# Moving 64 channels of the last convolution block to GpSimd, two halves at a time

## The chip, the cores and the metric

The kernel runs on one core of a Trainium2 chip. The metric is the device time of one execution in microseconds (us). The engines of the core run their own instruction streams in order and wait for each other through semaphores: TensorE (PE in the profile, its weight loads PEld), VectorE (DVE), ScalarE (ACT), GpSimd (POOL) and SyncE (SP), which here only issues DMAs.

## The reference

```python
# x: (8, 3904, 192), weight: (8 heads, 7 taps), w1, w2: (192, 1024), w3: (1024, 1024), w_out: (1024, 192)
w = softmax(weight)                                  # over the 7 taps of a head
x_pad = 6 zero rows ahead of each batch's 3904 rows
conv[b, s, h, g] = sum_k w[h, k] * x_pad[b, s + k, h, g]   # a causal convolution, 24 channels a head
out = ((conv @ w1) * (conv @ w2)) @ w3 @ w_out       # for all 31232 rows
```

## The kernel before, in words

**Tiling.** The 31232 rows are cut into two streams of 15616 (`NS = 2`), and each stream into 31 *rounds* of 512 columns (`CH`). The convolved x of a round is held transposed, with channels on partitions: three chunks `k = 0, 1, 2` of 64 channels, both streams stacked to 128 partitions. w3 and w_out are multiplied once at the start, so that a round has only two products:

- `first_product(R)` (L581): in 8 steps `ft` of 128 columns of w1 and w2, TensorE makes `pa` and `pb` (L596), ScalarE casts `pa` to `asb` (L603) and VectorE multiplies it by `pb` into `abT` (L605).
- `second_product(R, r)` (L615): for one stream, 32 matmuls into `ops` (L621), copied by ScalarE to `osb` (L626) and stored by SyncE (L635).

All PSUM results take turns in four tiles of two banks (`banks`).

**Stages.** Three rounds make a stage (the loop `for p, (rounds, ends)`, L863): first the three first products (24 steps), then the six second products, numbered `n = 0..5`. Other work is written into this order by hand. Two stages more at the end deal with the last rounds.

**Two ways to convolve.** Two rounds, 2q+1 and 2q+2, are a *pair* (`phase_of`, L56).

- *On TensorE*, for the pairs that are not in `SIDE`: x is loaded in blocks of windows (`x_jobs`, L137, DMAs of L158), multiplied by a banded matrix `Aband` in units of two heads (`conv`, L310, matmuls L328), evicted by ScalarE (L337), stored to DRAM as `rows` (`store`, L370) and read back by DMA transposes (`transposes`, L422). Blocks 4, 5 and 6 have 80 windows and four units each. `places` (L731) says after which second product of which stage a unit runs: `{0: (1, 2, 3, 4), 2: (0, 1, 3, 4), 4: (2, 4), 5: (1, 3)}`. Block 6, for the pairs 10 and 11, is in stages 4 and 5. x rows ahead of a batch are zeroed by GpSimd (`clear`, L857, memsets L860) once the x loads of a tile have been issued.
- *Beside it*, for the pairs in `SIDE`: a GpSimd DMA casts one chunk of x to `rows_c` (`side_cast`, L473, DMA L480), SyncE transposes it to `raw` (L489), and the seven taps are summed in fp32. Most of it is VectorE's: ScalarE makes the first product (`side_first`, L492), and VectorE adds six taps, one instruction each (`side_sums`, L498, L512), in the second half of a stage, `rooms` (L732) giving about how many sums a stage holds. Seven half-chunks of 512 columns are GpSimd's (`BY_POOL`, L450).

**GpSimd's halves.** Half number p of `BY_POOL` is cast in or before stage p, transposed by SyncE at the beginning of stage p's second half (`pool_transpose`, L531, L533) and summed in stage p + 1. `pool_sums` (L535) makes seven products (L539, `tensor_scalar`, the tap's weight a per-partition scalar; the first goes straight to `acc`) and six adds (L559, the last one L554). There is one `raw`, one `acc` and one `tmp`. The seven jobs are handed out one each to the `points` (L812) of a stage: a point (j, ft) lies behind step ft of the stage's round j, and GpSimd first makes a tiny copy `pace` from that step's abT (L876), so that it starts no sooner. Its DMAs (casts and x loads, `jobs`) are dealt to the same points by `counts` (L867).

**Queues.** An instruction that waits holds up all that is behind it on its engine. On SyncE, at the start of a second half, come transposes of `rows` that are due (`turn`), the side transposes of the next stage, GpSimd's transpose, and then the output stores; side transposes called `late` (L890) come after the output stores.

Of the kernel before, what the change touches and what calls it, by code (L numbers as in the profile page):

```python
# [8 lines left out]
FP32 = mybir.dt.float32  # L9
# [7 lines left out]
def kernel(  # L17
# [10 lines left out]
    nc = tc.nc  # L28
# [20 lines left out]
    SIDE = (4, 5, 8, 9, 12, 13, 14)  # L49
    SIZES = [20, 20, 20, 40, 80, 80, 80]  # L50
# [5 lines left out]
    def phase_of(R):  # L56
        return (R - 1) // 2

# [28 lines left out]
    def tok(i):  # L87
        return wins[i][0]

# [220 lines left out]
    def conv(b, c0, wd, evict=(nc.scalar.copy,), es=None):  # L310
        n, m, E = shape_of(b)
        es = range(E) if es is None else es
        if b not in convo_of:
            convo_of[b] = work.tile([128, n, NP, NS, Q], BF16, tag="convo", bufs=2,
                                    name="convo")
            left_of[b] = D * E
        convo = convo_of[b]
        cps = {e: banks("cps") for e in es}
        c = c0
        while c < c0 + wd:  # L320
            h = c // G
            c1 = min(h * G + G, c0 + wd)
            for j in range(4):
                xb, s = xb_of[b][j]
                for e in es:
                    for r in range(NS):
                        o = cps[e][j * C:j * C + C, r, 0:m * wd]
                        nc.tensor.matmul(  # L328
                            o.rearrange("p (w g) -> p w g", g=wd)[:, :, c - c0:c1 - c0],
                            Aband[group(r, e), h, :], xb[group(r, e), s:s + m, c:c1],  # L330
                            start=True, stop=True)
            c = c1
        for f, e in zip(evict, es):
            src = cps[e][:, :, 0:m * wd].rearrange("p r (w g) -> p r w g", g=wd)
            o = 0
            for k, lo, c in segments(c0, wd):
                f(out=convo[:, e::E, k, :, lo:lo + c]  # L337
                    .rearrange("p w r g -> p r w g"), in_=src[:, :, :, o:o + c])
                o += c
        left_of[b] -= wd * len(es)  # L340
        if not left_of[b]:
            del xb_of[b]
# [27 lines left out]
    def store(b, first=0, js=range(4)):  # L370
        n = SIZES[b] // 4
        convo = convo_of[b]
        for j in js:
            w = 0
            while w < n:
# [6 lines left out]
                elif s1 - s0 < ST:  # L382
                    m = 1
                    if s1:
                        nc.sync.dma_start(
                            out=rows[t + s0:t + s1, :],
                            in_=convo[C * j + s0:C * j + s1, w].rearrange("s k r g -> s (k r g)"))
                else:
                    src = convo[C * j:C * j + ST, w:w + m].rearrange("s w k r g -> s w (k r g)")
                    dst = rows[t:t + ST * m, :].rearrange("(w s) c -> s w c", s=ST)  # L390
# [31 lines left out]
    def transposes(R, first=0):  # L422
        t0, t1 = max(R * CH, first), min((R + 1) * CH, TS)
        a = ring_of[R] * CH % RING + t0 - R * CH
        for k in range(NP):
            nc.sync.dma_start_transpose(
                out=xT[k][:, a:a + t1 - t0], in_=rows[t0:t1, k * 128:(k + 1) * 128])
# [22 lines left out]
    BY_POOL = ((5, 2, 0), (5, 2, 1), (8, 2, 0), (8, 2, 1), (12, 2, 0), (12, 2, 1), (13, 2, 0))  # L450
# [69 lines left out]
    pool_raw, pool_acc, pool_tmp = [], [], const.tile([128, CH], FP32, name="tmp")  # L520

    def pool_tiles():
        t = stage.tile([128, 3 * CH + HALO], BF16, tag="wo", bufs=1, name="acc")
        pool_acc.append(t[:, 0:2 * CH].bitcast(FP32))
        pool_raw.append(t[:, 2 * CH:3 * CH + HALO])
# [5 lines left out]
    def pool_transpose(p, k, half):  # L531
        _, _, t0, _ = pool_half(p, k, half)
        nc.sync.dma_start_transpose(out=pool_raw[0], in_=rows_c[t0 - HALO:t0 + CH, k, :])  # L533

    def pool_sums(p, k, half):  # L535
        _, _, t0, starts = pool_half(p, k, half)

        def product(out, d):
            nc.gpsimd.tensor_scalar(  # L539
                out=out, in0=pool_raw[0][:, HALO - d:HALO - d + CH],  # L540
                scalar1=wC[:, k, K - 1 - d:K - d], scalar2=None, op0=ALU.mult)

        def job(d):
            def run():
                acc, tmp = pool_acc[0], pool_tmp
                if d == 1:
                    product(acc, 1)
                    for z in starts:
                        nc.gpsimd.memset(acc[:, z - t0:z - t0 + 1], 0.0)
                    return  # L550
                product(tmp, d)
# [10 lines left out]
        return [job(d) for d in list(range(1, K)) + [0]]  # L562

    def operand(R, k, rs):
        if phase_of(R) in side_of:
# [165 lines left out]
    places = {0: (1, 2, 3, 4), 2: (0, 1, 3, 4), 4: (2, 4), 5: (1, 3)}  # L731
# [43 lines left out]
    def later_loads():  # L775
# [9 lines left out]
        for i in starts[1]:  # L785
            for f in side_cast(i):
# [23 lines left out]
             for h in range(0, H, n)]  # L810
# [8 lines left out]
    pool_from = {p: v for p, v in enumerate(BY_POOL, 1)}  # L819
    pool_sum = {p + 1: pool_sums(*v) for p, v in pool_from.items()}  # L820
    casts = [(p - 1, f) for p in starts if p > 1 for i in starts[p] for f in side_cast(i)]
    casts += [(p, f) for p, (q, k, h) in pool_from.items()
# [40 lines left out]
    for p, (rounds, ends) in enumerate(phases):  # L863
# [3 lines left out]
        counts = [0] * 3 + [2] * 4 if p == 1 else [2] * 2 + [1] * 5  # L867
# [3 lines left out]
        for v, f in enumerate(pool_sum.pop(p, ())):  # L871
            at[v].append(f)
# [17 lines left out]
        late = [i for i in raws if p == 0 or i >= 5 and chain[p][0][0] <= i - 5]  # L890
# [55 lines left out]
```

## Time and profile before

| | us |
|---|---|
| runs | 511.17, 511.72, 512.06 (median 511.72) |
| the profiled execution | 510.92 |
| its span on the core | 509.2 |

The prediction shows lines of these views. *Engine totals*: busy us, share of the span and number of instructions of each engine. *The chain that ended last*: the work followed back from the last instruction, each step to what released it, as shares by engine, or as pieces in order of time (start, us, what). *Groups*: line, engine, operation, written tile <- read tiles, shapes, count | busy us, mean ns of one | idle us of the engine just before them and what ended that. *Timeline*: start, us from the first start to the last end of a run of like instructions, then the group, its count, and in brackets the idle time before it and who ended it. *DMA issues*: tile written <- tile read, queue, count, KB of one, median us from issue to landing.

### The profile page before, as it was taken

The numbers are of one execution on the slowest core, as the hardware profiler recorded it, in microseconds if no ns is written. First come the engines' busy times: TensorE is split into PE (matmuls) and PEld (weight loads), VectorE is DVE, ScalarE is ACT, GpSimd is POOL, SyncE is SP. The second block draws the span as 40 slices with busy tenths as digits, with TensorE's granted clock in tenths as the row PEclk, the third lists the DMA queues.
The fourth block names the chain that finished last, engine by engine and source line by source line (L and its number), as shares of the span: only waits on it lengthen the run. The fifth ranks groups of instructions, "written<-read, shape, count | busy, mean of one in ns | idle before, by whom it ended". The sixth has DMA issues, their size and how long they took to land.

```text
span 509.2 us, 13681 instructions
## 1 busy us (share of the span) xinstructions
PE 503.8 (99%) x5758; PEld 338.5 (66%) x5758; DVE 446.4 (88%) x402; ACT 347.2 (68%) x386; POOL 229.3 (45%) x303
## 2 busy tenths in 40 slices
PE   8999999999999999999999999999999999999997
PEld 4546864595569557845875596569557855965597
DVE  7898769999999799899989999999899999999930
ACT  6786667836778776477667767763776477457752
POOL 9966101333980597079519902970573067100000
PEclk9999999999999999999999999999999999999999
DMA  9999979999955999963889337975501400230024
GB/s 136 158 162 174 173 152 177 148 163 194 159 60 159 143 158 133 229 79 23 65 219 96 24 106 127 192 110 155 102 1 43 156 4 0 84 106 1 1 63 156
DMA packets 156825, 58.45 MB, mean 115 GB/s; under 512 B 112607, under 2 KB 156763, under 8 KB 156763
## 3 DMA queue, kind: packets, MB, share of 16 engines
q0 software_dynamic: 70560, 16.85, 37.2%
q1 hardware_dynamic: 86043, 40.62, 36.1%
q8 instruction: 45, 0.74, 0.6%
q14 instruction: 17, 0.14, 0.1%
q10 hardware_dynamic: 160, 0.10, 0.1%
HBM read 33.97 MB, written 34.85 MB: 135 GB/s over the span
## 4 chain that ended last, share of the span: by engine, by line
PE 98%; DMA 1%; ACT 0%; POOL 0%; DVE 0%; issue 0%; POOLq 0%
PE ops L621 32%; PE pa L596 31%; PE pb L596 31%; PE cps L328 1%; PE wps L693 1%; DMA xb<-in_x_dram 1%; PE tps L401 0%; PE ops L646 0%; PE tps L416 0%; DVE abT L605 0%; PE cps L357 0%; ACT asb L603 0%; POOL xb L158 0%; ACT convo L337 0%; ACT osb L650 0%
## 5 line engine op out<-in xcount | busy, mean ns | idle before, releaser
L605 DVE TENSOR_TENSOR abT<-asb,pb 128x1024 bf16<-128x1024 bf16 x240 | 292.7, 1221 | 30.4 <-ACT asb L603 14.5
L603 ACT CAST asb<-pa 128x1024 bf16<-128x1024 f32 x244 | 247.0, 1012 | 64.2 <-PE pa L596 64.0
L596 PEld LDWEIGHTS <-wn 64*128 64x128 bf16 x1488 | 138.5, 94 | 79.7 <-issue 1.6
L596 PEld LDWEIGHTS <-ws 64*128 64x128 bf16 x1488 | 129.7, 94 | 70.0 <-issue 1.4
L621 PE MATMUL ops<-W_sb,abT 128*128 128x192 bf16 x1936 | 163.7, 246 | 0.0
L621 PEld LDWEIGHTS <-abT 128*128 128x128 bf16 x1936 | 158.5, 98 | 6.4 <-issue 6.4
L596 PE MATMUL pb<-xT,wn 64*128 64x512 bf16 x408 | 111.2, 376 | 0.0
L596 PE MATMUL pa<-xT,wn 64*128 64x512 bf16 x408 | 110.1, 376 | 0.1
L596 PE MATMUL pa<-xT,ws 64*128 64x512 bf16 x408 | 110.1, 376 | 0.0
L596 PE MATMUL pb<-xT,ws 64*128 64x512 bf16 x408 | 108.5, 376 | 0.0
L626 ACT COPY osb<-ops 128x768 f32<-128x768 f32 (+1 forms) x61 | 48.5, 795 | 84.7 <-PE ops L621 82.3
L876 POOL COPY pace<-abT 1x2 bf16<-1x2 bf16 x57 | 10.9, 192 | 175.5 <-DVE abT L605 155.0
L596 PE MATMUL pb<-side,wn 64*128 64x512 bf16 (+1 forms) x336 | 88.8, 368 | 0.0
L596 PE MATMUL pa<-side,ws 64*128 64x512 bf16 (+1 forms) x336 | 87.3, 369 | 0.0
L596 PE MATMUL pa<-side,wn 64*128 64x512 bf16 (+1 forms) x336 | 87.3, 369 | 0.0
L512 DVE SCALAR_TENSOR_TENSOR acc<-raw,wC,acc 128x1024 f32<-128x1024 bf16 (+2 forms) x70 | 84.6, 1209 | 2.0
L596 PE MATMUL pb<-side,ws 64*128 64x512 bf16 (+1 forms) x336 | 85.7, 368 | 0.0
L539 POOL TENSOR_SCALAR tmp<-acc,wC 128x512 f32<-128x512 bf16 x42 | 65.8, 1566 | 1.2
L559 POOL TENSOR_TENSOR acc<-acc,tmp 128x512 f32<-128x512 f32 x35 | 44.4, 1267 | 2.9
L480 POOL DMA_DIRECT2D rows_c<-in_x_dram x50 | 37.1, 744 | 4.7 <-issue 2.7
L158 POOL DMA_DIRECT2D xb<-in_x_dram x50 | 32.2, 649 | 6.9 <-DMA xb<-in_x_dram 2.2
L512 DVE SCALAR_TENSOR_TENSOR acc<-side,wC,acc 128x1024 f32<-128x1024 bf16 (+1 forms) x20 | 24.3, 1217 | 3.8 <-ACT acc L494 3.2
(76 smaller groups left out, 186.9 us busy)
## 6 DMA issues: line engine op xcount, KB each, us to landing
out_dram<-osb SPq DMA_DIRECT2D x54, 384.0 KB
xb<-in_x_dram POOLq DMA_DIRECT2D x16, 240.0 KB, 7.2
out_dram<-osb SPq DMA_DIRECT2D x12, 192.0 KB
rows_c<-in_x_dram POOLq DMA_DIRECT2D x16, 130.0 KB, 5.6
rows_c<-in_x_dram POOLq DMA_DIRECT2D x12, 128.0 KB, 5.7
rows<-convo SPq DMA_DIRECT2D x6, 240.0 KB
xb<-in_x_dram POOLq DMA_DIRECT2D x6, 228.0 KB, 4.9
w3b<-in_moe_w_dram POOLq DMA_DIRECT2D x4, 256.0 KB, 5.5
```

What stands on the lines that cost most here:

```text
L158: nc.gpsimd.dma_start(out=tiles[js[0]][0][group(r, e), s:s + w, :], in_=bass.AP(tensor=x.tensor, offset=(r * TS + t - PAD) * D, ap=[[D, C] ...
L328: nc.tensor.matmul(o.rearrange("p (w g) -> p w g", g=wd)[:, :, c - c0:c1 - c0], Aband[group(r, e), h, :], xb[group(r, e), s:s + m, c:c1], ...
L480: nc.gpsimd.dma_start(out=rows_c[lo:t1, k, r * Q:r * Q + Q], in_=x_rows[r * TS + lo:r * TS + t1, k * Q:k * Q + Q])
L512: nc.vector.scalar_tensor_tensor(out=side_of[p][:, k, o:o + t1 - t0] if last else a, in0=raw[:, HALO + lo - t0 - d:HALO + hi - t0 - d], sc ...
L539: nc.gpsimd.tensor_scalar(out=out, in0=pool_raw[0][:, HALO - d:HALO - d + CH], scalar1=wC[:, k, K - 1 - d:K - d], scalar2=None, op0=ALU.mult)
L559: nc.gpsimd.tensor_tensor(out=a, in0=a, in1=tmp[:, lo - t0:hi - t0], op=ALU.add)
L596: nc.tensor.matmul(p[:, r, f * N:f * N + N], w_of(i, k, r)[rs, ft * 128:(ft + 1) * 128], operand(R, k, rs), start=(k == 0), stop=(k == NP ...
L603: nc.scalar.copy(out=asb[:, :, 0:per * N], in_=pa[:, :, 0:per * N])
L605: nc.vector.tensor_tensor(out=ab[:, f0, :, 0:N], in0=asb[:, :, 0:N], in1=pb[:, :, 0:N], op=ALU.mult)
L621: nc.tensor.matmul(ops[:, g // 2, (g % 2) * D:(g % 2) * D + D], ab[:, jt, r, g * 128:(g + 1) * 128], W_sb[:, jt, :], start=(jt == 0), stop ...
L626: nc.scalar.copy(out=osb.rearrange("p (a g) d -> p a (g d)", g=2), in_=ops[:, 0:ng // 2, 0:2 * D])
L876: P(out=pace, in_=abT_of[R][0:1, ft, 1, 0:2])
```

## The change

1. `PART = {10: (0,), 11: (0,)}`: chunk k = 0 (the first 64 channels) of the pairs 10 and 11 is convolved by GpSimd, in four more halves. `beside(q, k)` takes the place of the test for `SIDE`.
2. Block 6 loses chunk 0: `first_k(6) = 1`. Its units cover heads 2 to 7, three units instead of four; evictions, stores and transposes of chunk 0 are left out. `places` becomes `{0: (1, 2, 3, 4), 2: (0, 1, 3, 4), 5: (0, 2, 4)}`.
3. `POOL_AT` lists GpSimd's halves by the stage that sums them; stages 3 to 6 have two (*lanes*), each with a `raw` and an `acc` of its own and a common `tmp`. The four results lie in a tile that takes one of the five x buffers (`part_tile`).
4. ScalarE makes the first product of each half (`pool_first`), behind the fourth second product of the stage before; GpSimd then does six products and six adds. A product is a `tensor_tensor` with the weight broadcast along the columns.
5. In a stage with two lanes all sums stand at point (0, 0), lane 0 first, and all of the stage's DMAs at the last point, (2, 6); the side transposes of the next stage all become `late`. Casts for GpSimd's halves are due one stage sooner from the third on.

```diff
+    PART = {10: (0,), 11: (0,)}
+    def beside(q, k):
+        return q in SIDE or k in PART.get(q, ())
+    def first_k(b):
+        return min(k for k in range(NP) if not beside(phase_of(tok(FIRST[b] + 1) // CH), k))
...
-    BY_POOL = ((5, 2, 0), (5, 2, 1), (8, 2, 0), (8, 2, 1), (12, 2, 0), (12, 2, 1), (13, 2, 0))
+    POOL_AT = {2: ((5, 2, 0),), 3: ((5, 2, 1), (10, 0, 0)), 4: ((8, 2, 0), (10, 0, 1)),
+               5: ((8, 2, 1), (11, 0, 0)), 6: ((12, 2, 0), (11, 0, 1)), 7: ((12, 2, 1),),
+               8: ((13, 2, 0),)}
...
+    pool_more = const.tile([128, 3 * CH + HALO], BF16, name="acc")
+    def part_tile():
+        t = work.tile([128, XN], BF16, tag="xb", bufs=5, name="side")
...
+    def pool_first(lane, p, k, half):
+        nc.scalar.activation(
+            out=pool_acc[lane], in_=pool_raw[lane][:, HALO - 1:HALO - 1 + CH],
+            func=ACT.Copy, scale=wC[:, k, K - 2:K - 1])
...
-            nc.gpsimd.tensor_scalar(
-                out=out, in0=pool_raw[0][:, HALO - d:HALO - d + CH],
-                scalar1=wC[:, k, K - 1 - d:K - d], scalar2=None, op0=ALU.mult)
+                nc.gpsimd.tensor_tensor(
+                    out=tmp, in0=pool_raw[lane][:, HALO - d:HALO - d + CH],
+                    in1=wC[:, k, K - 1 - d:K - d].to_broadcast([128, CH]), op=ALU.mult)
...
-        return [job(d) for d in list(range(1, K)) + [0]]
+        return [job(d) for d in list(range(2, K)) + [0]]
...
-    places = {0: (1, 2, 3, 4), 2: (0, 1, 3, 4), 4: (2, 4), 5: (1, 3)}
+    places = {0: (1, 2, 3, 4), 2: (0, 1, 3, 4), 5: (0, 2, 4)}
...
-             for h in range(0, H, n)]
+             for h in range(first_k(b) * Q // G, H, n)]
...
-    casts += [(p, f) for p, (q, k, h) in pool_from.items()
+    casts += [(p if p < 3 else p - 1, f) for p, v in pool_from.items() for q, k, h in v
...
-        counts = [0] * 3 + [2] * 4 if p == 1 else [2] * 2 + [1] * 5
+        lanes = pool_sum.pop(p, ())
+        counts = [0] * 7 if len(lanes) > 1 else [0] * 3 + [2] * 4 if p == 1 else [2] * 2 + [1] * 5
...
-        for v, f in enumerate(pool_sum.pop(p, ())):
-            at[v].append(f)
+        for fs in lanes:
+            for v, f in enumerate(fs):
+                at[v if len(lanes) == 1 else 0].append(f)
...
-                              for v, (a, ft) in enumerate(points) if a == j and at[v]})
+                              for v, (a, ft) in enumerate(((0, 0),) + points[1:] if
+                                                          len(lanes) > 1 else points)
+                              if a == j and at[v]})
...
-        late = [i for i in raws if p == 0 or i >= 5 and chain[p][0][0] <= i - 5]
+        late = [i for i in raws if p == 0 or len(lanes) > 1 or i >= 5 and chain[p][0][0] <= i - 5]
...
-        if p in pool_from:
-            pool_transpose(*pool_from[p])
+        for lane, t in enumerate(pool_from.get(p, ())):
+            pool_transpose(lane, *t)
...
+            if n == 3:
+                for lane, t in enumerate(pool_from.get(p, ())):
+                    pool_first(lane, *t)
```

More of the change, by code (lines that the diff above doesn't have):

```diff
@@ L371, in store @@
         n = SIZES[b] // 4
-        convo = convo_of[b]
+        convo = convo_of[b][:, :, first_k(b):]
+        cols = slice(first_k(b) * NS * Q, NP * NS * Q)
         for j in js:
@@ L425, in transposes @@
         for k in range(NP):
+            if beside(phase_of(R), k):
+                continue
             nc.sync.dma_start_transpose(
```

45 lines of the change are left out of this document (25 added, 20 removed).

## The prediction

> **What bounds the kernel now.** I read the engine totals first, then the chain that ended last, then that chain in order of time, to see whether TensorE ever waits.
>
> ```profile
> PE 503.8 (99%) x5758; PEld 338.5 (66%) x5758; DVE 446.4 (88%) x402; ACT 347.2 (68%) x386; POOL 229.3 (45%) x303
> ...
> PE 98%; DMA 1%; ACT 0%; POOL 0%; DVE 0%; issue 0%; POOLq 0%
> ```
>
> ```profile
> 166.04 0.75 PE pa L596 x6
> ...
> 197.23 15.95 PE ops L621 x192
> 213.18 0.75 PE pa L596 x6
> ```
>
> TensorE holds 98% of the chain. Stage 3 is 166.04 to 213.18: 31.2 us of first products (24 steps), then 15.95 us of six second products, 47.1 us with no hole. So time can fall only by taking work from TensorE, and any new hole in it is lost. Next I asked how near the others are to making a hole, at the boundary of stages 4 and 5 (timelines of PE, then DVE).
>
> ```profile
> 244.30 8.09 PE L621 MATMUL ops<-W_sb,abT 128*128 128x192 bf16 x96
> 252.33 0.42 PE L328 MATMUL cps<-xb,Aband 32*32 32x240 bf16 x32
> ```
>
> ```profile
> 118.91 1.22 DVE L605 TENSOR_TENSOR abT<-asb,pb 128x1024 bf16<-128x1024 bf16 x1 [0.53 <-ACT asb L603]
> ...
> 245.94 1.28 DVE L512 SCALAR_TENSOR_TENSOR side<-raw,wC,acc 128x1024 bf16<-128x1024 bf16 x1
> ...
> 263.19 7.64 DVE L605 TENSOR_TENSOR abT<-asb,pb 128x1024 bf16<-128x1024 bf16 x6 [1.69 <-ACT asb L603]
> ```
>
> Stage 4 begins at 213.18, so VectorE starts its sums 32.8 us into a stage (245.94). In stages without a convolution, its first abT of the next stage waits only 0.53 us for ScalarE: that is all its cover. With two convolutions (0.42 us each) it is 1.69 us. TensorE itself bears about 0.3 us more: the third step's pb takes the first step's bank 2.6 us after the first pa ends, and cast and abT need 1.0 + 1.2. VectorE is thus the engine to watch, and GpSimd, 45% busy, matters through what it does to VectorE.
>
> **The change part by part.** Durations:
>
> ```profile
> L605 DVE TENSOR_TENSOR abT<-asb,pb 128x1024 bf16<-128x1024 bf16 x240 | 292.7, 1221 | 30.4 <-ACT asb L603 14.5 <-PE cps L328 0.3
> L603 ACT CAST asb<-pa 128x1024 bf16<-128x1024 f32 x244 | 247.0, 1012 | 64.2 <-PE pa L596 64.0
> L512 DVE SCALAR_TENSOR_TENSOR acc<-raw,wC,acc 128x1024 f32<-128x1024 bf16 x55 | 70.7, 1285 | 1.6
> L539 POOL TENSOR_SCALAR tmp<-acc,wC 128x512 f32<-128x512 bf16 x42 | 65.8, 1566 | 1.2
> L626 ACT COPY osb<-ops 128x768 f32<-128x768 f32 x60 | 48.0, 800 | 84.2 <-PE ops L621 82.3 <-DMA out_dram<-osb 1.8
> L559 POOL TENSOR_TENSOR acc<-acc,tmp 128x512 f32<-128x512 f32 x35 | 44.4, 1267 | 2.9
> L480 POOL DMA_DIRECT2D rows_c<-in_x_dram x50 | 37.1, 744 | 4.7 <-issue 2.7 <-DMA xb<-in_x_dram 1.9
> L220 POOL COPY ws<-wn 64x256 bf16<-64x256 bf16 x12 | 4.6, 396 | 0.5
> L494 ACT ACTIVATE acc<-raw,wC 128x512 f32<-128x512 bf16 x1 | 0.7, 724 | 0.0
> ```
>
> *Removed from TensorE:* one unit of 32 small matmuls, **-0.4 us**. That is the whole possible gain. ScalarE also drops four evictions, SyncE four transposes of rows and a third of the last block's bytes; all lie beside TensorE and are worth nothing. The new results take one of the five x buffers; the last block's loads then use buffers free since stage 0: nothing.
>
> *The product.* No two-tensor product with a broadcast operand is in the trace. The nearest rows are 1.27 us (the two-tensor add of the same 512 elements) and 1.57 us (the old product); far below lies a one-input copy, 0.396 us for 256 elements, so 0.8 for 512. I take 1.27, the row of the same kind of operation, and keep 0.8 and 1.57 as ends. The Trainium skill (GPSIMD Engine Reference, Engine selection) holds one-input operations at about line rate and two-input ones about twice slower. That speaks against this swap; here the one-input row is the slower, 1.57 against 1.27, so the row decides.
>
> *Two lanes in stages 3 to 6.* From operation to operation:
>
> ```profile
> 180.17 1.57 POOL L539 TENSOR_SCALAR tmp<-acc,wC 128x512 f32<-128x512 bf16 x1
> 181.82 1.27 POOL L559 TENSOR_TENSOR acc<-acc,tmp 128x512 f32<-128x512 f32 x1
> 183.04 0.17 POOL L876 COPY pace<-abT 1x2 bf16<-1x2 bf16 x1
> ```
>
> The add starts 0.08 after its product ends, the next operation 1.22 after the add's start: a tap is 1.27 + 0.08 + 1.22 = 2.57 us, a half of six taps 15.4, two halves 30.8. They start after the first abT (begun at 263.19, which is 2.1 us after stage 5's start at 213.18 + 47.1 + 0.84, and 1.22 long), at about 3.3, and end at 34.1, so the last add meets VectorE's sums. What a meeting costs, one place shows:
>
> ```profile
> 148.82 1.27 POOL L554 TENSOR_TENSOR side<-acc,tmp 128x512 bf16<-128x512 f32 x1
> 150.04 1.17 POOL L876 COPY pace<-abT 1x2 bf16<-1x2 bf16 x1
> ```
>
> ```profile
> 149.83 6.63 DVE L512 SCALAR_TENSOR_TENSOR acc<-raw,wC,acc 128x1024 f32<-128x1024 bf16 x5
> ...
> 157.86 6.57 DVE L512 SCALAR_TENSOR_TENSOR acc<-raw,wC,acc 128x1024 f32<-128x1024 bf16 x5
> ```
>
> A GpSimd copy that takes 0.17 us took 1.17, until VectorE's sum ended (149.83 + 1.3); and five sums that began under a GpSimd add took 0.06 longer. So GpSimd is held through a sum. Whether a sum is held through a whole GpSimd operation isn't shown: between 0 and 1.2 us each. I take 1.2, in turns: each GpSimd operation waits one sum (6.57 / 5 = 1.31) and each sum one operation. The Trainium skill (SBUF — State Buffer, Who interferes with whom) calls this an exclusive lock between a VectorE instruction with two SBUF inputs and a GpSimd one that reads SBUF; by it the upper end holds, and the row agrees for GpSimd's side.
>
> *Stage 3:* one operation late, GpSimd done at about 36.5; VectorE has only 11 sums there, so its cover is 0.53 + 1.3: **0**. Then all 16 of the stage's DMAs follow (before, they lay between the sums), and behind them the two memsets of the last block's zero rows, which wait for the last x load:
>
> ```profile
> 198.09 2.97 POOL L158 DMA_DIRECT2D xb<-in_x_dram  x5
> 207.51 0.25 POOL L860 MEMSET xb<- 6x192 bf16 x1 [1.45 <-DMA xb<-in_x_dram]
> ```
>
> ```profile
> xb<-in_x_dram POOLq DMA_DIRECT2D x16, 240.0 KB, 7.2
> rows_c<-in_x_dram POOLq DMA_DIRECT2D x16, 130.0 KB, 5.6
> ```
>
> Full casts come in pairs 0.75 us apart and land 5.6 us after issue, so one takes about 2.2 to 2.8; four full and four half casts are 13 to 17 us. The x loads are 80 windows, four times the 240 KB that land in pairs in 7.2, so 9 to 14. Together 18 to 28, and I take 23: from 36.6 the memsets end at 59.6, which is **12.5 us into stage 4**. There TensorE's program is already at its tenth step; GpSimd's sums should have begun at 3.3.
>
> *Stage 4* (12 sums, no convolution left): lane 0 from 12.6 to 28; lane 1 holds the batch boundary, its five middle adds are split, 16 us in all. At 32.8 some 11.2 us are left, about 9 whole operations and 3 small ones. In turns with the sums: 12 x 1.31 + 11 = 26.5, end at **59**. Now ScalarE's new first product of lane 1, placed after the fourth second product (about 41.7), needs that accumulator free and its raw tile transposed; SyncE's transpose waits for GpSimd's last product. Queued behind it on ScalarE are the last two osb copies and the next stage's casts: 59.1 + 0.7 + 0.8 + 0.8 + 1.0 puts the first abT at 62.4, against 49.2 (47.1 + 2.1): 13.2 late, less 0.3: **+13**. VectorE by itself would be 9 to 10 late. On SyncE the output stores queue behind that transpose, and the side transposes, moved to the stage's end, behind them; six output slots and the 31 us until their use hide that.
>
> *Stage 5.* After 59.5 GpSimd issues 6 x loads and 10 casts. A ninth DMA waits for the landing of the one eight before it:
>
> ```profile
> 26.84 0.54 POOL L662 DMA_DIRECT2D wo_b<-in_moe_w_out_dram  x1 [1.61 <-DMA xb<-in_x_dram]
> ```
>
> (that x load is the eighth one back; the idle time is 1.61 us). So the sixteenth goes out when six x loads (12) and two casts (4.5) are in, about 16 us later: 75.5, while stage 5 begins at 47.1 + 13 = 60.1. Sums start at 15.5; at 32.8, 13.5 us, 10.5 operations, are left: 10.5 x 1.31 + 13 = 27, end at 60. Behind ScalarE's wait stand the product 0.7, osb 0.8, an eviction 1.8, the late first product of task 11 1.15, osb 0.8, cast 1.0: abT at 66.3 against 47.1 + 3 x 0.42 + 2.1 = 50.5, less 0.3: **+15.5**. *Stage 6:* eight casts only, so the start is on time; one operation late, 1.2 less 0.8 of cover: **+0.4**.
>
> *Stage 2:* two new ScalarE products (0.72 each, 1.3 in sequence) go ahead of a convolution's evictions.
>
> ```profile
> 159.88 0.80 ACT L626 COPY osb<-ops 128x768 f32<-128x768 f32 x1 [1.36 <-PE ops L621]
> 160.57 1.95 ACT L337 CAST convo<-cps 128x640 bf16<-128x640 f32 x4
> 162.98 0.80 ACT L626 COPY osb<-ops 128x768 f32<-128x768 f32 x1 [0.45 <-PE ops L621]
> ```
>
> The evictions ended at 162.5 and would end at 163.8; four banks rotate, and the last second product takes that bank at about 162.95 + 0.42 = 163.4: **+0.45**. Elsewhere the two products lie in ScalarE's idle time between osb copies (1.36 above) and cost nothing, unless they wait.
>
> **Sum:** -0.4 + 0.45 + 0 + 13 + 15.5 + 0.4 = +29 on the profiled 510.92 (span 509.2): 539.9; the median of the runs shown, 511.72, is 0.8 above. I say **540**. The slack terms move it: memsets at 10 or 15 us instead of 12.5 change stage 4 to +7 or +17, the burst in stage 5 to +8 or +18; products at 1.57 (3.6 us more in a two-lane stage) add some 8.
>
> **The rivals.**
> - *No turn-taking:* the two engines hardly slow each other. For: sums grew only 0.06. Against: the copy's 1.17. Then stage 4 ends its sums at 44, ScalarE is ready at 46 and abT 0.5 late; in stage 5 the burst from 44 ends at T5 + 13, sums at 44, +1.7: 0.45 + 0.5 + 1.7 - 0.4 = +2.2, 514; with part of the cost up to 526.
> - *GpSimd on time in stage 4* (the burst lands early): only the last operations meet: stage 4 +1.2, stage 5 +0.3, stage 6 +0.4, stage 2 +0.45, less 0.4: 513.6. Against: 23 us of DMA behind a point at 36.
> - *Not slower, because the product is cheap:* at its lower end, 0.8 us, a tap is 2.1 and two lanes 25.2. Stage 3's sums end at 28.5, before VectorE's first sum; the DMAs leave at their own point, about 31.5, the memsets end at 54.5, 7.4 into stage 4, and lane 1 ends at 7.5 + 12.6 + 13.3 = 33.4, with one operation late. Stage 5 and 6 are then clear, and -0.4 to +0.4 remains: 511.3 to 512.1. It decides at about 0.9 us a product; above that, operations pile up behind 32.8. For: nothing excludes it. Against: the add's 1.27.
>
> **How the numbers follow.** A measurement tells about 0.2%, 1 us, from no change. Forecast (late in stages 4 and 5, in turns): 0.64, its own range 527 to 552. First two rivals together, 513 to 526: 0.19. Not slower: 0.17, of which 0.13 within 0.2% and 0.04 faster, since the gain is bounded by 0.4 us. Slower 0.83. The range 513 to 552 leaves out the not-slower case and a tail of slow products.
>
> **What would show it.** Right: GpSimd's first sum of stage 4 some 12 us into the stage after memsets waiting for x; VectorE's sums there doubling in spacing; ScalarE waiting for GpSimd or for the raw transpose; holes in TensorE at the ends of stages 4 and 5. Wrong: two-tensor products away from 1.27, memsets before 52, sums at 1.31 spacing beside running GpSimd operations, a PE chain as full as now.

## The result, and the profile after

The changed kernel takes 542.05 us (median of 6 runs, 539.45 to 544.35); the kernel before, run beside it, 511.47 (6 runs, 510.91 to 512.06). The ratio is 1.0594, 95% interval [1.0558, 1.0631]. The number and its sign were forecast (540, slower); two of the steps behind it were not, and they are the subject here. The profiled execution took 544.35 with a span of 542.6, so 33.4 us more span than before have to be found; it is the longest of the six. A *hole* is a time in which TensorE has no matmul to run. First the page of the changed kernel: engine totals, the granted clock in 40 slices, and the chain that ended last.

```profile
PE 510.5 (94%) x5726; PEld 341.2 (63%) x5726; DVE 461.4 (85%) x402; ACT 350.9 (65%) x393; POOL 275.5 (51%) x335
...
PEclk9999999996999999999979996899999999999999
...
PE 77%; POOL 12%; DMA 5%; ACT 2%; SPq 1%; issue 1%; DVE 0%; POOLq 0%; ACTq 0%; DVEq 0%
```

Before, TensorE held 98% of that chain. Now 23% of it lies elsewhere, and the clock line has three dips, each at a place where TensorE had stopped. VectorE has as many instructions as before (402) and is busy 15.0 us longer: its instructions have become slower.

To place the loss I took, for each stage, the time from its first `pa` matmul to its first `ops` matmul (first half), and from there to the next stage's `pa` (second half):

| stage | first half before | after | second half before | after |
|---|---|---|---|---|
| 1 | 31.18 | 31.19 | 15.95 | 15.94 |
| 2 | 31.19 | **41.99** | 17.78 | **18.33** |
| 3 | 31.19 | 31.19 | 15.95 | 15.95 |
| 4 | 31.19 | 31.19 | 16.87 | 15.94 |
| 5 | 31.24 | **38.33** | 16.87 | **29.78** |
| 6 | 31.25 | **33.63** | 15.94 | 15.95 |
| 7 | 31.25 | 31.24 | 15.95 | 15.95 |

The differences add up to 32.8. The rest is behind the last matmul: 3.6 us to the end of the span, where it was 3.0. Against the prediction:

| step | predicted | measured |
|---|---|---|
| the unit off TensorE | -0.4 | -0.5 (stage 4 -0.93; stage 5 +0.46, as e2_unit_only has it) |
| end of stage 1 | 0 | **+10.8** |
| stage 2, two products ahead of evictions | +0.45 | +0.55 |
| stage 3 | 0 | 0 |
| end of stage 4 | +13 | **+7.1** |
| end of stage 5 (12.5 in its own half, 2.4 in the next) | +15.5 | +14.8 |
| stage 6 | +0.4 | 0 |
| behind the last matmul | 0 | +0.6 |

So the forecast of the total is near by luck: a hole that it missed (10.8) and a hole that it made too large by 5.9 offset each other.

**The hole that was missed.** ScalarE's new product for stage 2 stands behind the fourth second product of stage 1. The waits of the changed kernel (us in total, times, longest) name what it waits for:

```profile
ACT acc L559 <- DMA acc<-rows_c: 36.5, 3, 15.2
PE pa L619 <- ACT osb L649: 25.5, 3, 12.4
...
POOL xb L883 <- DMA xb<-in_x_dram: 10.5, 1, 10.5
```

Three times ScalarE stands before L559, the new product, until a transpose into `raw` (here `acc`, the tile it is part of) lands, and three times TensorE stands before the first `pa` of a stage because ScalarE hasn't freed a bank. The first of the three, in ScalarE's timeline and in SyncE's:

```profile
111.75 0.80 ACT L649 COPY osb<-ops 128x768 f32<-128x768 f32 x1 [1.84 <-PE ops L644]
124.97 0.72 ACT L559 ACTIVATE acc<-acc,wC 128x512 f32<-128x512 bf16 x1 [12.43 <-DMA acc<-rows_c]
```

```profile
100.62 15.68 SPq L437 DMA_TRANSPOSE xT<-rows  x9
116.40 5.75 SPq L503 DMA_TRANSPOSE raw<-rows_c  x4
122.25 1.20 SPq L556 DMA_TRANSPOSE acc<-rows_c  x1
```

SyncE issues nine transposes of `rows` and four side transposes, 21.4 us of issuing, before it comes to GpSimd's. The two last `osb` copies and the casts of stage 2 queue behind the waiting product. This has nothing to do with the change of stages 3 to 6: the same order stands in SyncE's timeline of the kernel before,

```profile
100.16 14.58 SPq L426 DMA_TRANSPOSE xT<-rows  x9
...
120.92 1.21 SPq L533 DMA_TRANSPOSE acc<-rows_c  x1
```

where 120.92 comes 8.4 us after the place that the new product takes (behind the fourth `osb` copy, 111.75 + 0.80). There it did no harm, since GpSimd alone read that tile, in the next stage. The prediction worked out this wait for stages 4 and 5 only and wrote of all other places that the products "cost nothing, unless they wait".

**What a hole costs beyond itself.** TensorE's timeline, then pieces of the chain behind that hole:

```profile
126.43 0.58 PE L619 MATMUL pa<-xT,wn 64*128 64x512 bf16 x1 [8.04 <-ACT osb L649]
```

```profile
127.90 1.28 PE pb L619 x6
...
131.74 0.69 PE pa L619 x6
132.43 0.65 PE pb L619 x6
```

After 8.04 us without work a piece of six matmuls takes 1.28 us instead of 0.65, until 131.74: four pieces at half speed, 2.7 us, and 8.04 + 2.7 are the 10.8 of the table. The windows show the granted clock (last but two of the columns; PE, PEld, VectorE, ScalarE, GpSimd stand ahead of it) behind the first hole and in the third:

```profile
126.00:131.00 5.00, 4.57 (x22) 1.90 (x23) 2.44 (x2) 3.45 (x5) 0.18 (x1) 0.50 1.03 318
...
330.00:342.00 12.00, 2.38 (x12) 0.98 (x13) 6.39 (x4) 3.84 (x5) 11.70 (x12) 0.50 0.39 98
```

The Trainium skill (TensorE: Matmul & The Clock Gate, Part 1: The HAM clock gate) says that the clock drops to half after at least one idle window of about 3.4 us and rises after at least one of sustained work. The trace agrees: TensorE stopped at 118.39, the granted clock was 1.00 until 121.4 and 0.50 from 121.5 on, and it stayed at half from the restart at 126.43 to 131.74, 5.3 us.

**Stage 4.** GpSimd's timeline, from the memsets on:

```profile
236.11 0.56 POOL L883 MEMSET xb<- 6x192 bf16 x2 [10.47 <-DMA xb<-in_x_dram]
...
236.88 1.03 POOL L572 TENSOR_TENSOR tmp<-acc,wC 128x512 f32<-128x512 bf16 x1
237.99 1.26 POOL L582 TENSOR_TENSOR acc<-acc,tmp 128x512 f32<-128x512 f32 x1
239.33 1.04 POOL L572 TENSOR_TENSOR tmp<-acc,wC 128x512 f32<-128x512 bf16 x1
...
276.18 1.17 POOL L903 COPY pace<-abT 1x2 bf16<-1x2 bf16 x1
```

Stage 4 starts at 224.4, so the first sum comes 12.5 us in, as predicted, behind memsets that waited for the last x load (they end at 236.67, 59.4 us after stage 3's start at 177.2; predicted 59.6). But the product is 1.04 us, not 1.27, a tap 239.33 - 236.88 = 2.45 instead of 2.57, and the lanes end 51.8 us into the stage, not 59. ScalarE waits 8.88 us there, and TensorE's hole is 5.1 us (25.5 less 8.0 and 12.4); half clock behind it, until 281.9, makes it 7.1.

**Stage 5**, where the two engines meet all the way; GpSimd with its burst of DMAs, then VectorE:

```profile
277.29 3.82 POOL L165 DMA_DIRECT2D xb<-in_x_dram  x6
281.10 1.51 POOL L494 DMA_DIRECT2D rows_c<-in_x_dram  x2
285.12 0.78 POOL L494 DMA_DIRECT2D rows_c<-in_x_dram  x1 [2.50 <-DMA xb<-in_x_dram]
...
297.03 0.62 POOL L494 DMA_DIRECT2D rows_c<-in_x_dram  x1 [0.24 <-issue]
...
312.58 1.90 POOL L572 TENSOR_TENSOR tmp<-acc,wC 128x512 f32<-128x512 bf16 x1
314.56 2.13 POOL L582 TENSOR_TENSOR acc<-acc,tmp 128x512 f32<-128x512 f32 x1
...
337.56 0.41 POOL L903 COPY pace<-abT 1x2 bf16<-1x2 bf16 x2
```

```profile
311.48 2.10 DVE L526 SCALAR_TENSOR_TENSOR side<-raw,wC,acc 128x1024 bf16<-128x1024 bf16 x1
313.51 10.44 DVE L526 SCALAR_TENSOR_TENSOR acc<-raw,wC,acc 128x1024 f32<-128x1024 bf16 x5
...
326.07 10.42 DVE L526 SCALAR_TENSOR_TENSOR acc<-side,wC,acc 128x1024 f32<-128x1024 bf16 x5
```

Twelve sums and twelve GpSimd operations each take 25.0 us: lockstep, one for one, 2.09 us a pair (10.44 / 5). Alone they are 1.31 and, on the mean of product and add, 1.15; strictly in turns a pair would be 2.46. So a meeting costs a sum 0.78 us, inside the prediction's bounds of 0 and 1.2 and not at the end that it took.

### The profile page after: what moved, and what is told of

Read it like the earlier page. It is cut to its first block, busy times and chain, and to the rows that moved or that the text cites. A ratio compares the mean times of both kernels' runs of the same rounds, so it can differ in the third digit from the quotient of the medians.

```text
span 542.6 us, 13675 instructions
## 1 busy us (share of the span) xinstructions
PE 510.5 (94%) x5726; PEld 341.2 (63%) x5726; DVE 461.4 (85%) x402; ACT 350.9 (65%) x393; POOL 275.5 (51%) x335
## 4 chain that ended last, share of the span: by engine, by line
PE 77%; POOL 12%; DMA 5%; ACT 2%; SPq 1%; issue 1%; DVE 0%; POOLq 0%; ACTq 0%; DVEq 0%
PE pa L619 26%; PE pb L619 25%; PE ops L644 23%; POOL acc L582 5%; POOL tmp L572 5%; DMA xb<-in_x_dram 2%; DMA rows_c<-in_x_dram 2%; PE wps L716 1%; SPq L503 1%; DMA acc<-rows_c 1%; POOL side L577 1%; PE cps L335 1%; ACT convo L345 1%; DVE abT L628 0%; ACT osb L649 0%
## 5 line engine op out<-in xcount | busy, mean ns | idle before, releaser
L619 PE MATMUL pa<-xT,wn 64*128 64x512 bf16 x376 | 105.3, 384 | 13.2 <-ACT osb L649 13.2
L619 PE MATMUL pa<-side,wn 64*128 64x512 bf16 (+1 forms) x368 | 100.5, 373 | 12.4 <-ACT osb L649 12.4
L619 PE MATMUL pb<-xT,wn 64*128 64x512 bf16 x376 | 106.0, 382 | 0.0
L619 PE MATMUL pb<-xT,ws 64*128 64x512 bf16 x376 | 104.0, 382 | 0.0
L619 PE MATMUL pb<-side,wn 64*128 64x512 bf16 (+1 forms) x368 | 101.5, 371 | 0.5 <-DVE abT L628 0.5
L619 PE MATMUL pa<-side,ws 64*128 64x512 bf16 (+1 forms) x368 | 100.5, 373 | 0.0
L526 DVE SCALAR_TENSOR_TENSOR acc<-raw,wC,acc 128x1024 f32<-128x1024 bf16 (+2 forms) x70 | 93.1, 1330 | 8.0 <-ACT acc L508 6.0
L619 PE MATMUL pb<-side,ws 64*128 64x512 bf16 (+1 forms) x368 | 98.5, 371 | 0.0
L582 POOL TENSOR_TENSOR acc<-acc,tmp 128x512 f32<-128x512 f32 (+6 forms) x60 | 80.3, 1341 | 4.3
L572 POOL TENSOR_TENSOR tmp<-acc,wC 128x512 f32<-128x512 bf16 x66 | 76.6, 1160 | 3.5
```

Source lines behind the costliest of these rows:

```text
L526: nc.vector.scalar_tensor_tensor(out=side_of[p][:, k, o:o + t1 - t0] if last else a, in0=raw[:, HALO + lo - t0 - d:HALO + hi - t0 - d], sc ...
L572: nc.gpsimd.tensor_tensor(out=tmp, in0=pool_raw[lane][:, HALO - d:HALO - d + CH], in1=wC[:, k, K - 1 - d:K - d].to_broadcast([128, CH]), o ...
L582: nc.gpsimd.tensor_tensor(out=a, in0=a, in1=tmp[:, lo - t0:hi - t0], op=ALU.add)
L619: nc.tensor.matmul(p[:, r, f * N:f * N + N], w_of(i, k, r)[rs, ft * 128:(ft + 1) * 128], operand(R, k, rs), start=(k == 0), stop=(k == NP ...
```

## The experiments

**Theory.** All of the loss is order: ScalarE's product behind a transpose that SyncE issues late, and GpSimd's lanes behind DMAs and memsets that push them under VectorE's sums. **Rival 1:** the additional work as such costs, wherever it stands. **Rival 2:** it is ScalarE's wait that makes the holes, and the slowed sums matter little. Times of the kernel before in these comparisons are 510.9 to 511.6.

**e1_one_lane** takes the two-lane stages away and leaves the rest of the change.

```diff
-    POOL_AT = {2: ((5, 2, 0),), 3: ((5, 2, 1), (10, 0, 0)), 4: ((8, 2, 0), (10, 0, 1)),
-               5: ((8, 2, 1), (11, 0, 0)), 6: ((12, 2, 0), (11, 0, 1)), 7: ((12, 2, 1),),
-               8: ((13, 2, 0),)}
+    POOL_AT = {2: ((5, 2, 0),), 3: ((5, 2, 1),), 4: ((8, 2, 0),), 5: ((8, 2, 1),),
+               6: ((12, 2, 0),), 7: ((12, 2, 1),), 8: ((13, 2, 0),)}
```

> The changed kernel without the four new halves: GpSimd sums only the seven old ones, one lane. It leaves out chunk 0 of the pairs 10 and 11 altogether (old columns of xT stand in). Theory (ScalarE waits in order for a raw tile that comes late, in stage 1 because SyncE's queue is long, in stages 4 and 5 because GpSimd is late): the hole after stage 1 stays, about +10.8 us, the other holes go, less 0.4 for the unit: about 522, with one wait of ScalarE of 12 us for the raw transpose. Rival (VectorE's sums slowed by GpSimd make the holes): no collisions left here, 511 to 512.

520.66 us, ratio 1.0185 [1.0171, 1.0199]. Only stage 2's first half is long, 39.06; stages 4 and 5 show the unit, stage 6 has 31.49, and every other stage is as before. Its waits hold one of that kind:

```profile
ACT acc L558 <- DMA acc<-rows_c: 10.7, 1, 10.7
```

The missed hole is there without any second lane, and the lanes cost the remaining 21. It is smaller here, 7.9 us, and 7.7 in e4_memsets_later: SyncE came to the transpose at 120.58 and 119.44 instead of 122.25, TensorE stood for 6.3 and 5.3 us instead of 8.0, and half clock followed. So 10.8 is the hole of one execution, the longest.

**e3_early_transpose** issues that one transpose ahead of the second half's transposes in stage 1.

```diff
+        if p == 1:
+            pool_transpose(0, *pool_from[p][0])
         turn(p)
```

> The changed kernel with GpSimd's raw transpose of stage 1 put ahead of the nine transposes of rows and four side transposes on SyncE; nothing else. Theory: raw lands before 105 instead of 125, ScalarE's wait of 12.4 us goes, and with it the 10.8 us after stage 1: about 531. Rival (the DMA engines are full there and the tile is late anyway): ScalarE waits as long, 540 to 542.

535.05, ratio 1.0481 [1.0465, 1.0497], 4 us above the expectation; the profiled span falls from 542.6 to 532.5. Stage 2's first half is 31.19 again, stages 5 and 6 keep their holes (39.01, 28.78, 33.81). SyncE's timeline of this kernel, then ScalarE's:

```profile
104.99 1.12 SPq L556 DMA_TRANSPOSE acc<-rows_c  x1
106.21 10.78 SPq L437 DMA_TRANSPOSE xT<-rows  x6
```

```profile
113.94 0.72 ACT L559 ACTIVATE acc<-acc,wC 128x512 f32<-128x512 bf16 x1 [0.60 <-DMA acc<-rows_c]
```

Issued at 104.99, it lands only just in time, 8.9 us later and not before 105 as expected: the product waits 0.60 us for it instead of 12.43, between two osb copies, and TensorE loses nothing. The 10.1 us of span are, in the main, the 10.8 less 0.8 that this execution lost before stage 1. The medians differ by only 7.0. The profiled execution of the changed kernel was the longest of its six, which spread over 4.9 us, and that of this kernel the shortest of its four; a hole of 7.7 to 7.9, as in the two other profiles, would fit the 7.0 better, but those executions have no profile.

**e4_memsets_later** leaves out the memsets of the zero rows at the end of stage 3's first half; they come a stage later, as the block needs them only in stage 5.

```diff
-        clear()
+        if p != 3:
+            clear()
```

> The changed kernel with the two memsets behind stage 3's x loads put off to the end of stage 4. Theory: GpSimd starts its sums 3.3 us into stage 4 instead of 12.5, ends them near 33, the 7 us lost after stage 4 go; the burst of sixteen DMAs then starts near 35, ends 20 later, so stage 5's sums start about 8 in and the loss there falls from 15 to about 3 to 5: 521 to 526. Rival (two lanes collide with VectorE's sums whenever they run): stage 4 and 5 lose about as much, 537 to 542.

524.88, ratio 1.0272 [1.0253, 1.029]. Stage 5 has no hole (31.25, 17.32). What is left beside stage 2's 38.9 is stage 6's first half, 35.4: the casts of stage 4's end still keep GpSimd from stage 5's sums until 279.5, 11.3 us into it, and seven of VectorE's sums there meet the late lanes, these five among them:

```profile
302.72 10.44 DVE L526 SCALAR_TENSOR_TENSOR acc<-raw,wC,acc 128x1024 f32<-128x1024 bf16 x5
...
315.29 6.55 DVE L526 SCALAR_TENSOR_TENSOR acc<-side,wC,acc 128x1024 f32<-128x1024 bf16 x5
```

**e5_both** is the two edits together.

> The changed kernel with both mends at once: stage 1's raw transpose early and stage 3's memsets put off. Theory (three separate late starts, one of them left, the burst of sixteen DMAs ahead of stage 5): the two gains add up, 542 less 7 to 10 less 17, about 516 to 518; what stays is about 4 us after stage 5 and half a microsecond in stage 2. Rival (the holes share a cause, so one mend takes part of the other's gain): 521 or more.

517.92, ratio 1.0128 [1.0112, 1.0144]: the gains add (7.0 and 17.2; together 24.1). Left are stage 2's 18.33 and stage 6's first half, 36.88. That half is 1.5 longer than in e4_memsets_later, though TensorE's longest stop in it is the same (2.85 and 2.83 us): here the granted clock was 0.50 for 3.0 us behind the stop, there it stayed at 1.00.

**e6_x_sooner** is e3_early_transpose with the last block's x loads all in stage 2, so that no x load and no memset delays GpSimd in a two-lane stage. The order of the DMAs, and their number at the points of the one-lane stages, change with it.

```diff
-    for p, b, part, n in ((1, 5, 0, 0), (1, 5, 1, 4), (3, 6, 0, 0), (4, 6, 1, 0)):
+    for p, b, part, n in ((1, 5, 0, 0), (1, 5, 1, 4), (2, 6, 0, 0), (2, 6, 1, 0)):
```

> As the run with both mends, but the last block's fourteen x loads are issued in stage 2 instead of stages 3 and 4, so that stages 3 and 4 issue 8 and 10 casts only and the memsets fall in stage 2. Theory (GpSimd is late in stage 5 because its tenth to sixteenth DMAs wait for landings): its sums start 3.3 us into stage 5, the 4 us after stage 5 go: 511.5 to 513. Rival (two lanes end too late for VectorE even from 3.3): 515 to 517.

512.21, ratio 1.0016 [1.0005, 1.0027]. All the work of the change is in this kernel, the second lanes and the products on ScalarE included, and 30 us are gone. Rival 1 falls. Its stages are those of e2_unit_only, which has no second lane (31.49 in stage 6 there too), but for stage 2's second half, 18.33, and 0.2 us less in stage 8: placed right, the second lanes cost TensorE nothing that a stage shows, and ScalarE's products half a microsecond. GpSimd's first product of stage 4, which starts at 214.5, and VectorE's first sum there show that they come on time, and how close it is:

```profile
217.96 1.03 POOL L572 TENSOR_TENSOR tmp<-acc,wC 128x512 f32<-128x512 bf16 x1
```

```profile
247.34 1.86 DVE L526 SCALAR_TENSOR_TENSOR side<-raw,wC,acc 128x1024 bf16<-128x1024 bf16 x1
```

One sum meets one operation, 1.86 instead of 1.28, and no more. This is the case that the prediction held as its second rival (GpSimd on time in stage 4, 513.6).

**e7_no_scalar_product** is the changed kernel with GpSimd making the first product itself, so that ScalarE waits for nothing.

```diff
+                if d == 1:
+                    nc.gpsimd.tensor_tensor(
+                        out=acc, in0=pool_raw[lane][:, HALO - 1:HALO - 1 + CH],
+                        in1=wC[:, k, K - 2:K - 1].to_broadcast([128, CH]), op=ALU.mult)
...
-            if n == 3:
-                for lane, t in enumerate(pool_from.get(p, ())):
-                    pool_first(lane, *t)
```

> The changed kernel, but GpSimd makes the first product of each half itself (two more operations a stage with two lanes), so that ScalarE waits for no raw tile. Theory (in stages 4 and 5 ScalarE's wait and the slowed sums are late by about as much): the 10.8 us after stage 1 and the 0.5 in stage 2 go, the holes of stages 4 and 5 stay through VectorE, smaller by a third at most: 521 to 529. Rival (ScalarE's wait alone makes the holes): 512 to 515.

540.11, ratio 1.0559 [1.0541, 1.0576]: far above both expectations, and a miss of the theory as I had it. (GpSimd has two products more in a two-lane stage here, 2.1 us alone, so that a part of its lateness is this kernel's own.) The holes are now in the first halves of stages 5, 6 and 7 (37.91, 43.47, 42.05), and stage 2 is clean. VectorE, at the ends of stages 5 and 6:

```profile
302.70 10.67 DVE L526 SCALAR_TENSOR_TENSOR acc<-raw,wC,acc 128x1024 f32<-128x1024 bf16 x5
...
315.27 10.43 DVE L526 SCALAR_TENSOR_TENSOR acc<-side,wC,acc 128x1024 f32<-128x1024 bf16 x5
...
363.53 8.46 DVE L526 SCALAR_TENSOR_TENSOR acc<-raw,wC,acc 128x1024 f32<-128x1024 bf16 x4
```

The slowed sums alone are enough for a hole (TensorE's three long stops, 4.9, 9.3 and 7.9 us, all end with VectorE's abT); rival 2 falls with the expectation. And the wait on ScalarE had done something useful: in the changed kernel it holds TensorE until GpSimd has finished stage 5's lanes (337.56, and stage 6 starts at 339.6), so that stage 6 begins on time. Without it TensorE goes ahead (stage 6 starts at 316.4), GpSimd finishes the lanes of stage 5 only at 337.5, and its lateness is carried into stage 6, which then loses 10.8 at its end. This is read from the two timelines, with no run of its own. As I read it, a delay that one wait takes away comes back at the next meeting point as long as the late engine has no slack to catch up in.

**e8_fillers** measures the meeting by itself: the kernel before with ten operations of no use on GpSimd beside VectorE's sums, of three kinds in three stages.

```diff
+        def two():
+            nc.gpsimd.tensor_tensor(out=pool_tmp, in0=pool_tmp, in1=fill, op=ALU.mult)
+        def write():
+            nc.gpsimd.memset(pool_tmp, 1.0)
+        def one():
+            nc.gpsimd.tensor_copy(out=pool_tmp, in_=fill)
+        return [{6: two, 7: write, 8: one}[p]] * 10
```

> The kernel before with ten idle operations of GpSimd on 128x512 put beside VectorE's sums: two-input products in stage 6, write-only memsets in stage 7, one-input copies in stage 8. Theory (a sum and a GpSimd operation that reads SBUF take turns): in stage 6 both slow down to about 2.1 us each, VectorE ends 7 to 8 us late, 6 to 7 lost; in stage 7 sums stay at 1.31; in stage 8 copies slow the sums as products do. 518 to 526 in all. Rival (only two-input operations collide): stage 8 loses nothing, 517 to 518. Rival (no collision at all): 511.

520.54, ratio 1.0185 [1.0165, 1.0205]. GpSimd's timeline and VectorE's, stage by stage:

```profile
341.67 20.08 POOL L527 TENSOR_TENSOR tmp<-tmp,fill 128x512 f32<-128x512 f32 x10
...
396.73 5.76 POOL L530 MEMSET tmp<- 128x512 f32 x10
...
443.93 11.53 POOL L533 CAST tmp<-fill 128x512 f32<-128x512 bf16 x10
```

```profile
354.37 9.78 DVE L512 SCALAR_TENSOR_TENSOR acc<-raw,wC,acc 128x1024 f32<-128x1024 bf16 x5
...
397.76 6.56 DVE L512 SCALAR_TENSOR_TENSOR acc<-raw,wC,acc 128x1024 f32<-128x1024 bf16 x5
...
448.51 6.48 DVE L512 SCALAR_TENSOR_TENSOR acc<-raw,wC,acc 128x768 f32<-128x768 bf16 x5
...
456.19 5.22 DVE L512 SCALAR_TENSOR_TENSOR acc<-raw,wC,acc 128x768 f32<-128x768 bf16 x5
```

Beside two-input products a sum takes 1.96 in the mean of five (the last of them runs free), and stage 7's first half becomes 39.14, +7.9. Beside operations that only write, 1.31, as alone, and nothing is lost. Beside one-input copies the sums of 768 columns take 1.30 against 1.04, and stage 9's first half is 32.35, +1.1. The Trainium skill (SBUF — State Buffer, Who interferes with whom) says that a VectorE instruction with two SBUF inputs contends with a GpSimd one that reads SBUF and not with one that only writes. These three stages agree. The same section calls the contention an exclusive lock; held for whole instructions that would be the 2.46 a pair worked out above, and the trace has 2.09, so here some 0.4 us of each pair still overlap.

**e2_unit_only** is the kernel before with nothing but the first two points of the change, so that only the unit is taken off TensorE.

```diff
-    places = {0: (1, 2, 3, 4), 2: (0, 1, 3, 4), 4: (2, 4), 5: (1, 3)}
+    places = {0: (1, 2, 3, 4), 2: (0, 1, 3, 4), 5: (0, 2, 4)}
```

> The kernel before with only the one unit of the last block taken off TensorE; it leaves out chunk 0 of the pairs 10 and 11. Theory: the whole gain that the change could have is 32 small matmuls, 0.4 us: 511.1 against 511.5. Rival (a unit costs more than its matmuls, since evictions and banks hold TensorE around it): 1 us or more less.

511.86, ratio 1.0022 [1.0012, 1.0031]: a miss, not faster but slower by 0.2%. From the start of stage 4's second half to the start of stage 6 it takes 64.5 us against 65.0, so the half microsecond is there; stages 6 and 8 give 0.25 and 0.2 back. The profiled execution (its longest, 513.98) lost another 1.7 us before stage 1 and 1.4 behind the last matmul, to which e9_mended leads; how much the others lost before stage 1 isn't known.

**e9_mended** clears up what was left in e6_x_sooner (stage 2's second half 18.33, stage 6's first half 31.49); beside these lines, the halves (10, 0, 0) and (10, 0, 1) change places.

```diff
-    places = {0: (1, 2, 3, 4), 2: (0, 1, 3, 4), 5: (0, 2, 4)}
+    places = {0: (1, 2, 3, 4), 2: (0, 1, 3, 4), 5: (0, 1, 2)}
...
-            if n == 3:
+            if n == (2 if p == 2 else 3):
```

> The kernel of e6_x_sooner with what was left over in it moved: ScalarE's first products of stage 2 stand behind the third second product instead of the fourth, ScalarE's products of stage 5 stand at its first three places, and two GpSimd halves change places, so that stage 3 has the one with the batch boundary and stage 4 the one without. Theory (what is left in e6_x_sooner over the kernel before is 0.5 us at stage 2's end, 0.25 us in stage 6 and nothing else but the unit taken off TensorE): stage 2's second half goes back from 18.3 to about 17.8 us, and the time is 510.5 to 511.7, at best 0.4 us under the kernel before, and so no difference that five rounds tell apart for certain. Rival (the 0.5 us only moves to another pair of evictions, and the gain of the unit does not show, as it did not in e2_unit_only): 512 to 512.5.

511.72, ratio 1.0006 [0.9994, 1.0018]. The profile is as meant: stage 2's second half 17.79, every first half as before, stage 6 reached 238.95 us after stage 1's start where the kernel before needs 239.41. And yet the span is 509.5 against 509.2. The end shows why: nine of SyncE's last stores (two more follow), of the kernel before, then of this one.

```profile
496.51 9.34 SPq L635 DMA_DIRECT2D out_dram<-osb  x9
```

```profile
496.25 10.07 SPq L658 DMA_DIRECT2D out_dram<-osb  x9
```

Among these nine one is issued in 1.2 us instead of 0.46. In the kernel before and in e8_fillers it is the sixth from the end, and the next one waits for its data anyway: 3.0 us from the last matmul to the end. In the changed kernel and in all those above without the unit it is the fourth from the end, takes 1.14 to 1.71 us, and the last three go out late: 3.6 to 4.4 us (here 3.6; in e2_unit_only 4.4). That is the table's +0.6, and it eats what the unit saves.

**e10_split_store** and **e11_before_shifted** tried to move that slow store: e9_mended with one earlier output store in two pieces, and the kernel before with one earlier store handed to ScalarE.

```diff
+            if (R, r) == (22, 0):
+                for lo in (0, D // 2):
+                    hs = slice(lo, lo + D // 2)
+                    part = dict(out=args["out"][:, :, hs], in_=args["in_"][:, :, hs])
```

> e9_mended with one output store of stage 7 issued as two, each of half the 192 columns, so that SyncE has 512 more pieces to describe before its last stores. Nothing else changes. Theory (in the kernel before the sixth output store from the end takes 1.25 us to issue instead of 0.46, and its successor waits for its data anyway; in every kernel without the unit it is the fourth from the end, 1.14 to 1.71 us, and the last three stores go out 0.6 to 1.1 us later, behind the last matmul; the place depends on how much has been issued on that queue before): the long store moves away from the end, the span behind the last matmul falls from 3.6 to about 3.0 us, and the time is 510.4 to 511.2, some 0.6 us under e9_mended and 0.3 to 0.9 under the kernel before. Rival (the long issue comes from something else, such as the traffic of the last stores themselves): it stays on the fourth store from the end and the time stays that of e9_mended, 511.7.

511.81, ratio 1.0005 [0.9991, 1.002]. The slow store moved, but to the third from the end (1.11 us), where it does the same harm.

```diff
-            send = (nc.scalar if g and (R, r) == (NR - 1, NS - 2) else nc.sync).dma_start
+            send = (nc.scalar if g and (R, r) == (NR - 1, NS - 2) or (R, r) == (22, 0)
+                    else nc.sync).dma_start
```

> The kernel before with one output store of stage 7 issued by ScalarE instead of SyncE, so that SyncE has 512 pieces fewer to describe before its last stores, as it has fewer without the unit. Nothing else changes. Theory (the place of the long issue depends on what the queue has had before): it moves from the sixth store from the end to the fourth, and the time rises by 0.5 to 1.1 us over the kernel before, to about 512. Rival: the time and the place of the long store stay as they are, 511.2.

510.93, ratio 0.9987 [0.9978, 0.9997]. The slow store stayed sixth from the end (1.60 us), and nothing was lost. So the amount that the queue has had to describe before does not by itself set its place; the theory of both expectations falls. That the end takes 3.0 us with the slow store in the sixth place and 3.6 to 4.4 with it in the fourth or third held in the profiles of all 13 kernels of this study, one of each; what sets the place stays open, and so does whether the unit's half microsecond could be kept.

## Why the prediction was right, and where it was wrong

- **Slower, by about 29 us:** right, and for the main reason given, which is 21.9 of the 33.4 us: sums late behind loads and memsets, in lockstep with VectorE's, holes at the ends of stages 4 and 5. e4_memsets_later and e6_x_sooner took exactly that away and the holes went. That the total came within 3 us is luck: what it missed, a third of the profiled execution's loss, stood against a term that it made too large.
- **"Elsewhere the two products lie in ScalarE's idle time between osb copies ... and cost nothing, unless they wait":** this step failed. One of them waits 12.43 us, in stage 1, for a transpose that is 14th in SyncE's order; +10.8 in the profiled execution, 7.9 and 7.7 in two other profiles; that it is this wait is shown by e1_one_lane and e3_early_transpose. The prediction had the rule (a step that is placed ahead must find its input ready) and used it in two of the seven stages; the row that would have told it lies in the kernel before.
- **The collision, 1.2 us an operation:** mis-sized. In lockstep a sum loses 0.78. With the product at 1.04 instead of 1.27, which the prediction had named as a sign of being wrong, fewer operations were left when VectorE's sums began: stage 4 lost 7.1, not 13, and only 5.1 without the half clock. The row from which the lower bound was read could not tell: the five sums that took 0.06 longer began when the add beside them had 0.26 us left (148.82 + 1.27 - 149.83).
- **Stage 5, +15.5:** measured 14.8, by offsets. The burst of 16 DMAs took 297.03 + 0.62 - 277.29 = 20.4 us, not 16. So GpSimd began only 13.7 us ahead of VectorE's first sum, at 311.48, where 17.3 were predicted, and 12 operations were left instead of 10.5; but the lockstep was cheaper than turns.
- **Half clock after a hole:** not in the sum at all. It is 2.7 of the 10.8 in stage 2; in the other two holes it is part of the measured 7.1 and 14.8, about 1.9 of each.
- **The unit, -0.4:** -0.5 where it stood. The prediction took it as gained to the end of the kernel; the end of the kernel gave 0.6 back.
- **The third rival** (not slower, because the product is cheap, below 0.9 us): it didn't apply, at 1.04. Whether a product below 0.9 us would have been enough no run shows. e6_x_sooner shows another switch: at the same 1.04 us the loss goes when no x load stands ahead of the sums.

## What to carry to other kernels

Before you place an instruction earlier on an in-order engine, read for each stage, not for the worst ones only, when its input is issued and landed today: the issue queue (here SyncE, 1.1 to 1.8 us for each transpose), and the landing (2.7 us after the issue here, 8.9 in e3_early_transpose) are part of that time. When a slow engine and a busy one slow each other down, count how many operations of the slow one are left when the busy one starts, times what a pair costs. The lateness, not the amount of work, decided between 542 and 512 here. And look past the hole: a lateness that no slack absorbs comes back one stage on, and after the holes of 4.9 us and more TensorE started again at half speed.

## What the runs showed of the hardware

- A two-tensor product of 512 bf16 elements with a broadcast second input takes 1.04 us on GpSimd, the two-tensor fp32 add 1.27, and the product with a per-partition scalar that it replaces 1.57.
- VectorE's sums (1.31 us) and GpSimd's two-input operations go in lockstep at 2.09 us a pair; one-input copies cost a sum of 768 columns 0.25; write-only memsets (0.58 us each) cost it nothing.
- After the first hole of 8.04 us TensorE ran at half clock for 5.3 us. A stop of 2.85 us was followed by 3.0 us of half clock in e5_both, one of 2.83 in e4_memsets_later by none.
- With 16 DMAs in a row on GpSimd's queue the ninth (285.12 in stage 5) is the first to wait until an x load has landed, 2.50 us; the 16, six x loads and ten casts, took 20.4 us.
- One store in the last six on SyncE's queue takes 1.1 to 1.7 us to issue instead of 0.46, at a place that differs between kernels for a reason not found; in 9 of the 13 profiles the fourteenth from the end is slow as well.
